# A convolution feeding a channel mix: how the later groups' x is loaded, when their units run, and when their output is written

## The chip, the cores and the metric

The kernel runs on one core of a Trainium2 chip. The metric is device time in microseconds, from the launch of the program to its end, as the median over several runs. TensorE (PE in the profile) multiplies, ScalarE (ACT) and VectorE (DVE) take results out of PSUM and do the elementwise work, GpSimd (POOL) and SyncE (SP) mostly issue DMAs.

## The reference, cut to what matters

```python
# first part: x (8, 4160, 192), weight (8 heads, 7 taps)
w = softmax(weight, axis=-1)
x_pad = concat(zeros(6 rows), x)                       # causal
y[b, s, head] = sum_k w[head, k] * x_pad[b, s + k, head]   # 24 channels per head
# second part, on y
y_prev = y shifted by one row
xk = mu_k * y + (1 - mu_k) * y_prev
xr = mu_r * y + (1 - mu_r) * y_prev
k = relu(xk @ w_k)                                     # 192 -> 1024
out = sigmoid(xr @ w_r) * ((k * k) @ w_v)              # 1024 -> 192
```

A depthwise causal convolution of seven taps, shared within each of eight heads, runs along the sequence. Its output goes through a channel mix: two blends of each row with the row before it, a 192 to 1024 to 192 network with a squared relu, and a sigmoid gate.

## The kernel before, in words

**Tiling.** The eight sequences are taken as four pairs p. A *step* is 512 rows of both sequences of a pair (there are 34, with short ones at the ends of the first pair and a last one for the tails). A step's k part is cut into *slots*, and four slots make a *bundle*: there are 65, and a step is two of them. Everything is issued by hand (`manual_schedule`): a loop over bundles b calls `bundle_first`, `bundle_second`, `bundle_third` and then `bundle_rest` for each. Each engine and each DMA queue runs its instructions in the order in which they are issued.

**A bundle** (`bundle_rest`). PE does four `k_mm` (ps_k, L591, 6 matmuls each), one `r` (ps_r, L648), one `v_rows` in two halves (ps_v, L679), and in some bundles a convolution unit. ACT does four `k_relu` (L603), one sigmoid (L659), and casts of the unit. DVE does four squares (L617), `v_out` (o_sb, L695) of the bundle before, and the blends: `diff` (d, L534), `scale` (L565), `add_y` (L571). `v_out` also has SP issue two DMAs to the output (L703). All PSUM results share one ring of four two-bank tiles, tag "k".

**Tables.** What a bundle does beside this stands in tables of calls by bundle: `early` runs ahead of the bundle, then `mix_a`, `mix_b` (after the first two k_mm), `mix_c`, and `late` at the end; `xt` holds the convolution units. `at(table, b, fn, ...)` adds a call.

**Groups.** The convolution is done in groups of blocks of rows. The first pair has six groups of other shapes (0 to 5). Pairs 1 to 3 have two groups each, 6 to 11, called *sparse*: 20 blocks of 4 x 26 rows, done with 32x32 matmuls (L362). `fb` is the bundle in which a group's first rows enter the channel mix; for groups 6 to 11 it is 16, 24, 32, 40, 48, 56. A sparse group goes through these stages:

1. `x_tile(g)` takes the next of two xb tiles and has DVE write two elements of it (L123), which waits for the tile's former users. `load_x(g, (s,))` has POOL issue four DMAs (L152) for sequence s, one for each quarter of the partitions, that read x in fp32 and write bf16. Before the second sequence, `tie_x` has DVE write two elements (L111) that the first of its DMAs overwrites, so that POOL waits for DVE to reach that place.
2. Four units c (`conv_sparse`), each with 32 matmuls over two PSUM tiles, and then ACT's casts (`cast_tiles`, L335) into two y tiles, one half of the rows each. The y tiles come from a pool of two, so the next group's first casts take the same two.
3. `y_write(g)` has SP issue eight DMAs (L464) that write y to a buffer in DRAM, four for each half.
4. `y_read` has SP issue two transposing DMAs (L486), one for each half of the rows, into yT, which `diff` reads from bundle fb - 2 on.

`keep_tail(p)` (y_tail, L518) copies the last rows of a pair's yT on POOL, in POOL's queue with the x loads.

**SP's queue** has all output writes, y writes and transposes in one order. After the last unit of a sparse group it holds: eight y writes, two output DMAs of the next `v_out`, two of the one after, the first transpose.

Of the kernel before, what the change touches and what calls it, by code (L numbers as in the profile page):

```python
# [14 lines left out]
def kernel(  # L15
# [11 lines left out]
    nc = tc.nc  # L27

    B, S, D = x.shape
# [11 lines left out]
    TB = 26  # L41
# [38 lines left out]
    n = 0  # L80
# [9 lines left out]
    groups = []  # L90
    for p in range(NPAIR):
        base = 0
        for nb, s, on_pe in (
# [4 lines left out]
            if on_pe is None:  # L98
                base = min(base, S - nb * 4 * TB)
# [3 lines left out]
    sparse = {g for g, grp in enumerate(groups) if grp[4] is None}  # L103
# [2 lines left out]

    xbs, homes = {}, {}

    def tie_x(g, s):

        nc.vector.memset(xbs[g][0:1, 1, s, 0:2], 0.0)  # L111

    def x_tile(g):
        p, base, nb, _, on_pe = groups[g]
# [12 lines left out]
            n0 = nb - (base + 2 * nb * HB - S) // HB - 1  # L127
            nc.gpsimd.memset(xb[Q:P, n0:nb, :, :], 0.0)

    def load_x(g, batches=range(2)):  # L130
        p, base, nb, _, on_pe = groups[g]
        xb = xbs[g]
        if on_pe:
            parts, step, rows = ((0, base),), BLK, P
        elif g in sparse:
            parts, step, rows = [(32 * i, base + i * nb * TB) for i in range(4)], TB, 32
        else:
            parts, step, rows = ((0, base), (Q, base + nb * HB)), HB, Q
        for s in batches:
            b = 2 * p + s  # L140
            for q0, start in parts:
                lo, hi = 0, nb
                t0 = start - HALO
                if t0 < 0:
                    lo = 1
                    nc.gpsimd.dma_start(out=xb[HALO:rows, 0, s, :], in_=x[b, 0 : rows - HALO, :])
                while t0 + (hi - 1) * step + HALO + step > S:
                    hi -= 1
                    r0 = t0 + hi * step
                    if r0 + HALO < S:  # L150
                        nc.gpsimd.dma_start(out=xb[q0 : q0 + S - r0, hi, s, :], in_=x[b, r0:S, :])
                nc.gpsimd.dma_start(  # L152
                    out=xb[q0 : q0 + rows, lo:hi, s, :],
                    in_=bass.AP(
                        tensor=x.tensor,
                        offset=x.offset + (b * S + t0 + lo * step) * D,
                        ap=[[D, rows], [step * D, hi - lo], [1, D]],
                    ),
                )
# [21 lines left out]
    n = groups[0][2] * 2 * D  # L181
# [118 lines left out]
    ys, yTs, y_drams = {}, {}, {}  # L300
# [149 lines left out]
    def new_yT(p):  # L450
        yTs[p] = two.tile([P, 3, -(-(YC + S) // 16) * 16], BF16, tag="yT", name="yT")
        y_drams[p] = dram.tile([NROW, 2 * D], BF16, tag=f"y{p % 2}", name="y_dram")
        nc.vector.memset(yTs[p][:, :, 0:YC], 0.0)


    def y_write(g):
        p, base, nb, _, _ = groups[g]
        if base == 0:
            new_yT(p)
        if g in sparse:  # L460
            m = nb // 4
            for half in range(2):
                for j in range(4):
                    nc.sync.dma_start(  # L464
                        out=bass.AP(
                            tensor=y_drams[p].tensor,
                            offset=y_drams[p].offset + (base + (2 * half * nb + j) * TB) * 2 * D,
                            ap=[[2 * D, TB], [4 * TB * 2 * D, 2 * m], [1, 2 * D]],
                        ),
                        in_=ys[g][half][32 * j : 32 * j + TB, :, :],  # L470
                    )
            return
        m = nb // 2
        for i in range(2):
            for j in range(2):
                r0 = base + (i * nb + j * m) * HB
                nc.sync.dma_start(
                    out=y_drams[p][r0 : r0 + m * HB, :].rearrange("(n t) c -> t n c", t=HB),
                    in_=ys[g][j * Q : j * Q + HB, i * m : (i + 1) * m, :],
                )  # L480

    def y_read(g, part=slice(0, 1), of=1):
        p, base = groups[g][:2]
        n = (ends[g] - base) // of
        r0, r1 = base + part.start * n, base + part.stop * n
        nc.sync.dma_start_transpose(  # L486
            out=yTs[p][:, :, YC + r0 : YC + r1], in_=y_drams[p][r0:r1, :]
        )
# [242 lines left out]
    early, rq, rs, xt, mix_a, mix_b, mix_c, vq, late = ({} for _ in range(9))  # L731

    def at(table, b, fn, *a):
        table.setdefault(b, []).append((fn, a))
# [7 lines left out]
    for g, (p, base, nb, fb, on_pe) in enumerate(groups):  # L742
        if g < 3:
            continue
        if p == 0:
            xs = {3: [1, 1], 4: [2, 2, 3, 3], 5: [4, 4, 5, 5]}[g]
        else:
            xs = {6: [7, 8, 9, 10], 7: [12, 13, 15, 17]}.get(g, [fb - 13, fb - 11, fb - 9, fb - 7])
        for i, b in enumerate(xs):
            xt.setdefault(b, []).append((g, i))  # L750
        if not on_pe:
            at(late, xs[-1], y_write, g)
        if g in sparse:
            at(late, max(fb - 5, xs[-1] + 2), y_read, g, slice(0, 1), 2)
            at(late, fb - 2, y_read, g, slice(1, 2), 2)
            b, b1 = {6: (3, 5), 7: (7, 9), 8: (15, 16), 9: (24, 25)}.get(g, (fb - 19, fb - 16))
            table = mix_c if g == 7 else early
            at(table, b, x_tile, g)
            at(table, b, load_x, g, (0,))
            table = mix_c if g == 6 else early  # L760
            at(table, b1, tie_x, g, 1)
            at(table, b1, load_x, g, (1,))
            continue
        if not on_pe:
            if g == 4:
                at(mix_c, 4, y_read, g, slice(0, 1), 2)
                at(late, 4, y_read, g, slice(1, 2), 2)
            else:
                at(late, 6, y_read, g)
        if g > 4:  # L770

            at(mix_a, 1, x_tile, g)
            at(mix_a, 1, load_x, g)
    for s, (p, t0, L, n0, ns) in enumerate(steps):
        fb = first_bundle[s]
# [27 lines left out]
    for s, j, vb in quads:  # L803
        b = vb - (s == LAST)
# [261 lines left out]
```

## Time and profile before

| | |
|---|---|
| median of 3 runs | 410.98 us (410.81 to 411.77) |
| profiled execution | 409.68 us |
| its span | 407.9 us |
| PE busy | 400.9 us, 98% |
| PE weight loads busy | 303.7 us, 74% |
| DVE busy | 369.5 us, 91% |
| ACT busy | 354.7 us, 87% |
| POOL busy | 57.9 us, 14% |
| moved by DMA | 66.23 MB, mean 162 GB/s |

The span is from the first to the last instruction that the profile holds; the execution is 1.8 us longer. Busy time is the union of an engine's instructions, DMA issues not counted. In lists of waits the numbers are the total in microseconds, how often, and the longest; in the chain and the timelines, the start, the duration and what ran, with how many instructions were put together.

### The profile page before, as it was taken

What the parts mean: (1) busy time and instruction counts of PE and PEld (TensorE: products, weight loads), DVE (VectorE), ACT (ScalarE), POOL (GpSimd) and SP (SyncE); (2) the same over time, 40 slices, a digit from 0 to 9 for tenths busy, and PEclk for the clock granted to TensorE, in tenths of its full rate; (3) what the DMA queues carried; (4) which work ended last, traced back from release to release, by engine and by line L of the source; (5) the groups of instructions that cost most, each with busy time, mean ns of one, the idle gap of its engine ahead of it and who ended that gap; (6) DMA issues with size and microseconds to landing.
All of it is one profiled execution on the core that took longest, in us unless ns stands there. A gap on an engine that the chain in (4) does not pass through costs nothing.

```text
span 407.9 us, 17547 instructions
## 1 busy us (share of the span) xinstructions
PE 400.9 (98%) x7736; PEld 303.7 (74%) x7736; DVE 369.5 (91%) x672; ACT 354.7 (87%) x426; POOL 57.9 (14%) x91
## 2 busy tenths in 40 slices
PE   8899999999999999999999999999999999999996
PEld 5667777767878777777777777777777778777795
DVE  5999899988999999999999999999999899999973
ACT  6899989989988898988898898889899877877781
POOL 8731223000700003104020013000000001000000
PEclk9999999999999999999999999999999999999999
DMA  9999999999997758999995896969623946221223
GB/s 151 188 204 227 191 213 208 219 215 193 161 192 208 169 125 140 221 221 187 192 166 141 224 184 126 167 179 213 120 80 97 218 119 159 79 77 43 80 80 116
DMA packets 138955, 66.23 MB, mean 162 GB/s; under 512 B 89356, under 2 KB 138880, under 8 KB 138880
## 3 DMA queue, kind: packets, MB, share of 16 engines
q1 hardware_dynamic: 95536, 48.20, 47.6%
q0 software_dynamic: 42544, 16.36, 34.9%
q8 instruction: 60, 0.98, 1.0%
q10 hardware_dynamic: 800, 0.57, 0.5%
q14 instruction: 15, 0.12, 0.1%
HBM read 33.29 MB, written 36.86 MB: 172 GB/s over the span
## 4 chain that ended last, share of the span: by engine, by line
PE 93%; ACT 1%; issue 0%; DVE 0%; ACTq 0%
PE ps_v L679 42%; PE ps_k L591 40%; PE ps_r L648 8%; PE ps_c L362 2%; PE ps_v L631 1%; ACT k_sb L603 1%; PE ps_c L317 0%; ACT y L437 0%; PE ps_c L391 0%; DVE o_sb L715 0%; ACTq L399 0%; ACTq L603 0%
## 5 line engine op out<-in xcount | busy, mean ns | idle before, releaser
L603 ACT ACTIVATE k_sb<-ps_k 128x1024 bf16<-128x1024 f32 x260 | 253.4, 1039 | 34.0 <-PE ps_k L591 33.2
L617 DVE TENSOR_TENSOR k<-k_sb 128x1024 bf16<-128x1024 bf16 x260 | 173.4, 688 | 25.7 <-ACT k_sb L603 25.7
L591 PE MATMUL ps_k<-xk,wk 64*128 64x512 bf16 (+1 forms) x1632 | 192.1, 367 | 0.9 <-DMA wk<-in_moe_w_k_dram 0.9
L679 PE MATMUL ps_v<-wv,k 64*128 64x192 bf16 x4032 | 188.8, 243 | 0.2
L679 PEld LDWEIGHTS <-k 64*128 64x128 bf16 x4032 | 168.6, 94 | 12.7 <-issue 5.0
L591 PEld LDWEIGHTS <-wk 64*128 64x128 bf16 x1632 | 84.8, 94 | 55.1 <-issue 1.4
L695 DVE TENSOR_TENSOR o_sb<-ps_v,r_sb 128x768 f32<-128x768 f32 x64 | 60.9, 951 | 2.7 <-issue 2.4
L152 POOL DMA_DIRECT2D xb<-in_x_dram x62 | 43.9, 714 | 135.4 <-DVE xb L111 48.8
L659 ACT ACTIVATE r_sb<-ps_r 128x768 bf16<-128x768 f32 x65 | 53.5, 825 | 7.7 <-PE ps_v L679 5.6
L335 ACT CAST y<-ps_c 128x960 bf16<-128x960 f32 (+2 forms) x84 | 52.6, 709 | 0.0
L648 PEld LDWEIGHTS <-xr 64*128 64x128 bf16 x780 | 35.0, 94 | 14.1 <-issue 0.4
L648 PE MATMUL ps_r<-wr,xr 64*128 64x192 bf16 x780 | 43.3, 243 | 0.0
L565 DVE TENSOR_SCALAR xr<-d,mu 128x512 bf16<-128x512 bf16 (+1 forms) x102 | 35.0, 347 | 0.0
L534 DVE TENSOR_TENSOR d<-yT 128x1536 bf16<-128x1536 bf16 (+4 forms) x36 | 31.2, 866 | 1.1 <-ACT yT L421 1.0
L571 DVE TENSOR_TENSOR xr<-xr,yT 128x1536 bf16<-128x1536 bf16 (+1 forms) x33 | 31.1, 942 | 1.1
L565 DVE TENSOR_SCALAR xk<-d,mu 128x512 bf16<-128x512 bf16 (+1 forms) x99 | 31.7, 350 | 0.1
L571 DVE TENSOR_TENSOR xk<-xk,yT 128x1536 bf16<-128x1536 bf16 (+3 forms) x33 | 30.5, 924 | 0.1
L518 POOL COPY y_tail<-yT 128x195 bf16<-128x195 bf16 x4 | 3.5, 868 | 89.5 <-DMA yT<-y_dram 89.5
L362 PEld LDWEIGHTS <-toe 32*32 32x32 bf16 x768 | 5.0, 88 | 10.3 <-issue 8.9
L362 PE MATMUL ps_c<-xb,toe 32*32 32x240 bf16 x768 | 10.9, 267 | 0.0
L125 POOL MEMSET xb<- 32x384 bf16 x3 | 1.2, 408 | 61.5 <-PE ps_v L679 34.2
L411 PE MATMUL ps_t<-toe,xb 128*32 128x120 bf16 (+3 forms) x264 | 5.4, 238 | 0.2 <-ACT yT L421 0.2
(60 smaller groups left out, 61.9 us busy)
## 6 DMA issues: line engine op xcount, KB each, us to landing
out_dram<-o_sb SPq DMA_DIRECT2D x128, 192.0 KB
xb<-in_x_dram POOLq DMA_DIRECT2D x52, 240.0 KB, 8.2
y_dram<-y SPq DMA_DIRECT2D x48, 195.0 KB
y_dram<-y SPq DMA_DIRECT2D x8, 210.0 KB
xb<-in_x_dram POOLq DMA_DIRECT2D x6, 228.0 KB, 4.6
xb<-in_x_dram POOLq DMA_DIRECT2D x4, 192.0 KB, 6.0
wk<-in_moe_w_k_dram POOLq DMA_DIRECT2D x4, 192.0 KB, 5.8
wv<-in_moe_w_v_dram POOLq DMA_DIRECT2D x1, 384.0 KB, 8.4
```

What stands on the lines that cost most here:

```text
L152: nc.gpsimd.dma_start(out=xb[q0 : q0 + rows, lo:hi, s, :], in_=bass.AP(tensor=x.tensor, offset=x.offset + (b * S + t0 + lo * step) * D, ap ...
L335: nc.scalar.copy(out=bass.AP(tensor=y.tensor, offset=y.offset + d, ap=[y.ap[0], [m * 2 * D, 2], [2 * D, m], [Q, 2], [1, b - a]],), in_=bas ...
L534: nc.vector.tensor_tensor(out=shaped(s, diffs[s][:, cs, :L]), in0=y_of(s, cs, 1), in1=y_of(s, cs, 0), op=ALU.subtract)
L565: nc.vector.tensor_scalar(out=t[:, c, :L], in0=diffs[s][:, c, :L], scalar1=mu[:, i, c : c + 1], scalar2=None, op0=ALU.mult)
L571: nc.vector.tensor_tensor(out=o, in0=o, in1=y_of(s, sl, 0), op=ALU.add)
L591: nc.tensor.matmul(out=ps[:, i, f * L : (f + 1) * L], lhsT=wk[r, c, fs], rhs=xk[r, c, :L], start=c == 0 and f == 0, stop=c == NC - 1 and f ...
L603: nc.scalar.activation(out=k_sb, in_=ps.rearrange("p a b -> p (a b)"), func=AF.Relu)
L617: nc.vector.tensor_tensor(out=o, in0=i, in1=i, op=ALU.mult)
L648: nc.tensor.matmul(out=ps[:, i, k * D : (k + 1) * D], lhsT=xr[q, c, ts], rhs=wr[q, c, :], start=c == 0, stop=c == NC - 1,)
L659: nc.scalar.activation(out=r_sbs[s, j], in_=r_ps.pop((s, j))[:, :, 0 : 2 * D], func=AF.Sigmoid)
L679: nc.tensor.matmul(out=v_ps[s, j][:, bank, k * D : (k + 1) * D], lhsT=k2s[s][q, f, t * P : (t + 1) * P], rhs=wv[q, f, :], start=half == 0 ...
L695: nc.vector.tensor_tensor(out=o_sb.rearrange("p (b t) d -> p b (t d)", b=2), in0=v_ps.pop((s, j)), in1=r_sbs.pop((s, j)), op=ALU.mult,)
```

## The change

Three things change for groups 6 to 11.

- x: the load is cut into its eight DMAs. `load_part(g, s, i)` has DVE write two elements of quarter i of sequence s, and POOL issue that quarter's DMA. Two parts are called in each of four consecutive bundles, one in `early` and one in `mix_b`. The start is bundle 3, 7, 14 for groups 6, 7, 8 and fb - 18 for the rest (before: two calls of four DMAs, at 3 and 5, 7 and 9, 15 and 16, 24 and 25, and fb - 19 and fb - 16).
- Units: group 6 stays at 7 to 10; the others are at fb - 12, fb - 10, fb - 8, fb - 6 (before: 12, 13, 15, 17 for group 7, and fb - 13, fb - 11, fb - 9, fb - 7).
- y: `y_write_half` writes one half with four DMAs, in `late` of fb - 6 and of fb - 5 (before: both halves in `late` of the last unit's bundle). The transposes are called at fb - 4 and fb - 2 (before: fb - 5, or 12 for group 6, and fb - 2).

```diff
-    def tie_x(g, s):
-
-        nc.vector.memset(xbs[g][0:1, 1, s, 0:2], 0.0)
+    def load_part(g, s, i):
+
+        nc.vector.memset(xbs[g][32 * i : 32 * i + 1, 1, s, 0:2], 0.0)
+        load_x(g, (s,), slice(i, i + 1))
...
-    def load_x(g, batches=range(2)):
+    def load_x(g, batches=range(2), which=slice(None)):
...
-            for q0, start in parts:
+            for q0, start in parts[which]:
...
+    def y_write_half(g, half):
+        p, base, nb, _, _ = groups[g]
+        if base == 0 and half == 0:
+            new_yT(p)
+        m = nb // 4
+        for j in range(4):
+            nc.sync.dma_start(
+                out=bass.AP(
+                    tensor=y_drams[p].tensor,
+                    offset=y_drams[p].offset + (base + (2 * half * nb + j) * TB) * 2 * D,
+                    ap=[[2 * D, TB], [4 * TB * 2 * D, 2 * m], [1, 2 * D]],
+                ),
+                in_=ys[g][half][32 * j : 32 * j + TB, :, :],
+            )
...
-            xs = {6: [7, 8, 9, 10], 7: [12, 13, 15, 17]}.get(g, [fb - 13, fb - 11, fb - 9, fb - 7])
+            xs = [7, 8, 9, 10] if g == 6 else [fb - 12, fb - 10, fb - 8, fb - 6]
...
-        if not on_pe:
+        if on_pe is False:
             at(late, xs[-1], y_write, g)
         if g in sparse:
-            at(late, max(fb - 5, xs[-1] + 2), y_read, g, slice(0, 1), 2)
-            at(late, fb - 2, y_read, g, slice(1, 2), 2)
-            b, b1 = {6: (3, 5), 7: (7, 9), 8: (15, 16), 9: (24, 25)}.get(g, (fb - 19, fb - 16))
-            table = mix_c if g == 7 else early
-            at(table, b, x_tile, g)
-            at(table, b, load_x, g, (0,))
-            table = mix_c if g == 6 else early
-            at(table, b1, tie_x, g, 1)
-            at(table, b1, load_x, g, (1,))
+            for half in range(2):
+                at(late, fb - 6 + half, y_write_half, g, half)
+                at(late, fb - 4 + 2 * half, y_read, g, slice(half, half + 1), 2)
+            b = {6: 3, 7: 7, 8: 14}.get(g, fb - 18)
+            at(early, b, x_tile, g)
+            for n in range(8):
+                at((early, mix_b)[n % 2], b + n // 2, load_part, g, n // 4, n % 4)
             continue
```

More of the change, by code (lines that the diff above doesn't have):

```diff
@@ L459, in y_write @@
             new_yT(p)
[L460 to L472, printed above, removed]
         m = nb // 2
```

## The prediction

> **What bounds the kernel now.** I read the page first: its busy row, slices and chain.
>
> ```profile
> span 407.9 us, 17547 instructions
> PE 400.9 (98%) x7736; PEld 303.7 (74%) x7736; DVE 369.5 (91%) x672; ACT 354.7 (87%) x426; POOL 57.9 (14%) x91
> ...
> DMA  9999999999997758999995896969623946221223
> ...
> PE 93%; ACT 1%; issue 0%; DVE 0%; ACTq 0%
> ```
>
> PE is busy 98% and makes up 93% of the chain, so time is lost only where PE is made to wait. The DMA engines are nearly full for the first 70% of the span, but nothing in the chain is a DMA. Next, PE's own waits:
>
> ```profile
> PE warm L851 <- DVE ones_t L830: 1.5, 1, 1.5
> PE ps_k L591 <- DMA wk<-in_moe_w_k_dram: 0.9, 2, 0.5
> PE ps_t L411 <- ACT yT L421: 0.2, 1, 0.2
> PE ps_c L317 <- ACT k_sb L603: 0.2, 1, 0.2
> ```
>
> That is the whole list, 2.8 us, all of it before bundle 4: the 32x32 groups make PE wait nowhere. Busy PE need not be PE at its peak, so I read its pace from the chain of waits in order of time. A run of 18 ps_k matmuls opens each bundle:
>
> ```profile
> 186.00 1.94 PE ps_k L591 x18
> ...
> 192.20 2.00 PE ps_k L591 x18
> ...
> 197.98 1.94 PE ps_k L591 x18
> ...
> 204.18 2.00 PE ps_k L591 x18
> ...
> 317.46 1.94 PE ps_k L591 x18
> ...
> 323.21 1.94 PE ps_k L591 x18
> ```
>
> Bundles take 6.20 and 5.78 us in turn where every second one holds a unit, and 5.74-5.75 at the end where none does and DMA is quiet. A pair with a unit takes 11.98, so a unit costs 11.98 - 2 x 5.74 = 0.50 us, its own matmuls (0.35-0.50 in the chain, and a few hundredths of slower ps_v). There is no wait in the loaded stretch to give back. Here the Trainium skill speaks for more room: "Trainium Kernel Development and Optimization", Performance Expectations, says that matmul busy time is a bad measure and weight-load busy a good one. By it, 74% leaves a quarter to gain. By the pace, identical with DMA full and with DMA quiet, there is about none. I take the pace.
>
> Last, the engines around one hand-over of the y tiles (group 9's last unit, then group 10's first), from the timelines of SP, ACT and PE:
>
> ```profile
> 216.31 7.41 SPq L464 DMA_DIRECT2D y_dram<-y  x8
> 223.82 2.97 SPq L703 DMA_DIRECT2D out_dram<-o_sb  x4
> 226.83 4.47 SPq L486 DMA_TRANSPOSE yT<-y_dram  x1
> ```
> ```profile
> 215.33 1.82 ACT L335 CAST y<-ps_c 128x960 bf16<-128x960 f32 x2
> ...
> 227.25 1.82 ACT L335 CAST y<-ps_c 128x960 bf16<-128x960 f32 x2
> ```
> ```profile
> 215.99 2.11 PE L591 MATMUL ps_k<-xk,wk 64*128 64x512 bf16 x18
> ```
>
> SP issues eight y writes, about 0.95 us each[...], then two out pairs, then the transpose. The casts of the next group's first unit, 11.9 us later, write the same two y tiles (pool of two) and must wait for those writes. The PE row matters as much: its 18 matmuls are three ps_k tiles of 0.65 us (a run of six in the chain), so the third starts at 217.29; the PSUM ring has four tiles and this one takes the tile that the second cast has just left (215.33 + 1.82 = 217.15). PE's margin behind that cast is 0.14 us.
>
> **The change, part by part.**
>
> *Memsets.* Eight ties per sparse group instead of one, six groups: 42 more DVE memsets at 59 ns (the tile view of xb) = 2.5 us of DVE over 24 loading bundles, two to a bundle. DVE is busy 44.3 of 47.8 us between 198.66 and 246.46, so 0.5 us more fits the 3.5 idle. The work that is put back by 0.06-0.12 us is the square, xk and o_sb; xk of the next step is ready at 202.3 and first read at 204.18, 1.9 us later (0.7 in a bundle without a unit). Cost 0; if that cover is gone, 0.12 us a loading bundle, 2.5 in all.
>
> *x in eight parts.* The same 62 transfers, 0.69 us each on POOL's queue, now each behind its own memset. The first waits for the previous tenant's loads as before. The last part goes out in the middle of bundle b+3, three bundles before the unit in the general case, against a landing of 7.8 us median and 14.4 at most: covered. The tight one is group 6: last part in bundle 6 (memset near 48 us, issued to 49), unit at 56.96. Before, the four DMAs behind the memset at 44.23 landed 5.2 to 8.9 us after issue, the last at 55.6. Now the others are already through, so I expect 54-56: nothing, bound 0 to 1 us. On POOL, y_tail of pair 0 moves between group 8's parts; the yT it needs is tens of us old there. Queue neighbours of the y writes change little: x is clear of them either way, except at group 6, where one or two parts are in flight before and after.
>
> *Units.* Groups 7 to 11 move by 0 or 1 bundle, so pairs stay pairs. Group 7's first two units no longer stand side by side: bundles 12 to 18 take 6.20, 6.33, 5.73, 6.40, 5.78, 6.48, 5.73 in the chain, 42.65 - 7 x 5.74 = 2.47 for four units, against 4 x 0.50. Gain 0 to 0.5; I take 0.3. In the even bundles DVE carries a little more (o_sb, xr, d), but the long bundle gives it 0.45 us more.
>
> *y_read.* SP's order was y x8, out, out, transpose; it becomes y x4, out, y x4, out, transpose. The same twelve DMAs stand ahead of the transpose, so it starts 9.7-10.8 us after the last cast as before and lands 17-18 after it (before: 226.83 + 4.47, landing counted at 234.9 by the trace's semaphore records). But units end one bundle nearer to the reader, d (L534) in bundle fb-2: 5.7 + 6.2 + 5.7 to its first relu and 2.7 into it = about 20 us after the cast, where it was 26. Margin 2-3 us, no cost taken.
>
> *y_write in halves.* This is where I see a price. The second half goes out "a bundle later", but SP is paced by its queue: the first four writes keep it until about 3.1 us after the cast, then the out pair of the next v_out, whose o_sb is ready by then, then at once the second four. What changes is one out pair ahead of four of the eight writes: the pair's issues took 1.3, 1.4, 1.3, 1.9 and 2.7 us (with their semaphore waits 1.4, 1.5, 1.4, 2.0, 2.8) in the five hand-overs. Bound below: the pair is free in the queue, 0. Nothing in the trace shows a second half behind a pair, so I use the landing records: the eighth y write landed at 88.61, 131.56, 179.75, 227.11 and 275.80, and the second cast that needs it began at 89.86, 132.50, 180.29, 228.09 and 275.90, so the slack was 1.25, 0.94, 0.54, 0.98, 0.10. With the pair's issue time added, it is late by 0.1, 0.6, 0.9, 1.0, 2.7; by the landing of the tenth DMA instead (88.61 becomes 89.67; 132.74; 180.82; 229.30; 276.77) by -0.2, 0.2, 0.5, 1.2, 0.9. Less PE's margin of 0.14 each: 4.7 us and 2.3 us. The rule that stands here is in "DMA: Bandwidth & Descriptors", Anatomy of one DMA: about 2.0 us plus bytes over 436 GB/s, given there for the GpSimd path, which makes 2.5 us for a 195 KB write. The trace has 3.2 to 4.1 us from the end of the eighth issue to its landing, behind a full queue. With the rule the lateness falls by 0.7-1.6 each and about 1.0 us is left; I keep the trace. ACT catches up from its idle time (0.82 + 0.21 a pair), PE cannot: it has none. I take 2.7.
>
> Sum: -0.3 + 0 + 0 + 2.7 = +2.4 us on the profiled 409.7 (407.9 span and 1.8 around it). The median of the runs is 410.98, 1.3 above the profiled execution; I add the difference to it: 413.4.
>
> **Rivals.** *It lands in time (0.30).* Without x beside them the writes drain faster, and the out pair costs less than the slack of 0.1-1.25 plus 0.14. Then only the spacing is left, -0.5 to 0: 410.5-411.0, no change. For it: the slack is real in four of five places, and DMA is only 0.74 busy between 268 and 272 us. Against: SP's 0.95 us a write[...]. It decides at a second half that lands under 11.9 us after the first half's issue began; 12.1-12.3 is my reckoning.
>
> *A late input (0.08).* Group 6's last part stops PE at bundle 7, or the transpose misses d: each microsecond past a 2-3 us margin, four times, goes through DVE to xk and PE. 414-418.
>
> *Faster (0.07).* Timed runs are 1.3 us above the profiled one; if that is DMA bursts that the profile did not catch, spreading x would give part of it back: 409.5.
>
> That the parts are not spread at all is unlikely: POOL did wait for the ties, six times, 48.8 us in all.
>
> **How the numbers follow.** Forecast, the late second half: 0.55, 411.8 to 416.0. A measurement tells about 0.3% from nothing, 1.2 us. Of the forecast 0.03 falls inside that, so slower is 0.52 + 0.08 = 0.60, same 0.33, faster 0.07. The range goes from the no-change case with its gain, 410.2, to the upper sum, 416.0.
>
> **What would show it.** Right: ACT idle before L335 casts, released by the DMA y_dram<-y, up to five times, 0.2-2 us, all in first units, and PE waiting for ACT at ps_k right after; SP rows of four y writes with two outs between. Wrong: no such wait and pairs still at 11.95; or waits of PE or DVE on xb or yT instead.

## The result, and the profile after

The changed kernel takes 430.52 us, the median of six runs (427.14 to 436.09), against 410.89 for the kernel before in the same comparison (six runs, 410.65 to 414.08): a ratio of 1.0454, interval 1.0394 to 1.0514. It is slower by 19.6 us, where 2.4 had been forecast. Every kernel here has some executions more than 1.5% above its fastest; the ratios leave these out, and where a median below contains some, the times behind its ratio stand beside it. The profiled execution took 433.16 us with a span of 431.5, so it is 2.6 us above the median; the accounts below are of this execution, against the 407.9 us of span before.

The head of the page of the changed kernel: span, busy row, chain by engine.

```profile
span 431.5 us, 17622 instructions
...
PE 404.4 (94%) x7736; PEld 304.2 (71%) x7736; DVE 375.0 (87%) x714; ACT 355.6 (82%) x426; POOL 57.0 (13%) x91
...
PE 49%; DVE 21%; DMA 9%; ACT 6%; SPq 5%; issue 5%; DVEq 0%; ACTq 0%
```

PE's busy time grew by only 3.5 us while the span grew by 23.6, so PE now waits for some 20 us. It makes up 49% of the chain that ended last, where it was 93%, and DMA, which had no share at all, has 9%. What PE waited for (total, how often, longest):

```profile
PE ps_k L594 <- ACT y L336: 6.9, 5, 1.7
PE ps_k L594 <- DVE xk L574: 5.4, 1, 5.4
PE ps_v L682 <- issue: 3.1, 3, 1.6
PE ps_k L594 <- DMA wk<-in_moe_w_k_dram: 2.4, 3, 1.0
PE ps_r L651 <- DVE o_sb L698: 1.7, 1, 1.7
```

The first row is the predicted wait, at all five hand-overs of the y tiles. The second is a single wait of 5.4 us, of a kind that the prediction gave a chance of 0.08. The third has no releaser in the profile; the last section comes back to it. To place them I measured each bundle from the start of its first relu to that of the next, before and after:

| bundles | before, us | after, us | difference |
|---|---|---|---|
| ahead of bundle 0 | 11.41 | 12.57 | +1.2 |
| 6 | 5.67 | 13.58 | +7.9 |
| 7 to 10 | 25.31 | 29.89 | +4.6 |
| 12, 20, 28, 36, 44 (hand-overs) | 5 x 6.38 | 40.14 | +8.2 |
| 32 | 6.48 | 7.50 | +1.0 |

For the hand-overs and bundle 32, the column "before" has the undisturbed length in a kernel with the units of the changed one (a_y_whole_x67 below). The rows make 22.9 of the 23.6 us. The first belongs to no part of the change: the code is the same there, PE waits for the load of wk, and the kernels of the experiments show 12.0 to 12.7 there whatever they change.

The row of bundles 7 to 10 needs the same caution, since "before" is one execution. Four kernels below have the code of the kernel before up to bundle 10 (b_units, b_y_halves, b_y_halves_pool, b_x8_parts); they take 26.2 to 29.6 us there, and in each `d` waits 1.6 to 3.2 us for group 5's transpose. So 0.9 to 4.2 us can be lost in these bundles without any change to them.

Elsewhere the pace is the old one. The chain of waits in order of time, of the changed kernel, has the same runs of 18 ps_k matmuls 6.20 and 5.77 us apart in turn:

```profile
310.84 1.94 PE ps_k L594 x18
317.04 2.00 PE ps_k L594 x18
322.81 1.94 PE ps_k L594 x18
```

So two places carry the loss: the hand-overs of y (8.2) and bundles 6 to 10 (12.5, of which 7.9 in bundle 6).

**A hand-over.** Group 9 to group 10 again, timelines of SP, ACT and PE of the changed kernel (start, duration, what ran, idle time before it and its releaser):

```profile
242.03 3.00 SPq L476 DMA_DIRECT2D y_dram<-y  x4
245.14 2.67 SPq L706 DMA_DIRECT2D out_dram<-o_sb  x2
247.91 3.90 SPq L476 DMA_DIRECT2D y_dram<-y  x4
251.91 2.69 SPq L706 DMA_DIRECT2D out_dram<-o_sb  x2
254.63 3.83 SPq L489 DMA_TRANSPOSE yT<-y_dram  x1
```
```profile
252.98 0.95 ACT L336 CAST y<-ps_c 128x960 bf16<-128x960 f32 x1
255.82 0.96 ACT L336 CAST y<-ps_c 128x960 bf16<-128x960 f32 x1 [1.89 <-PE ps_k L594]
```
```profile
253.64 1.46 PE L594 MATMUL ps_k<-xk,wk 64*128 64x512 bf16 x12
256.83 0.82 PE L594 MATMUL ps_k<-xk,wk 64*128 64x512 bf16 x6 [1.73 <-ACT y L336]
```

The order on SP is the predicted one, and PE stops at the third ps_k tile of the bundle, behind the second cast, as was worked out from the PSUM ring. The cast starts 4.0 us after the last y issue ended (251.81 to 255.82). Its idle time is put down to PE, whose matmuls had ended at 255.10; in two of the five it is put down so, in the other three to the DMA `y_dram<-y`. The releaser is inferred, and the edits below decide which it is.

**Bundles 3 to 6.** SP's queue, the kernel before and then the changed kernel:

```profile
35.06 2.69 SPq L477 DMA_DIRECT2D y_dram<-y  x4
37.85 1.60 SPq L703 DMA_DIRECT2D out_dram<-o_sb  x2
39.56 4.00 SPq L486 DMA_TRANSPOSE yT<-y_dram  x2
...
47.79 2.09 SPq L477 DMA_DIRECT2D y_dram<-y  x4
```
```profile
36.35 2.61 SPq L465 DMA_DIRECT2D y_dram<-y  x4
39.06 3.34 SPq L706 DMA_DIRECT2D out_dram<-o_sb  x2
42.51 11.67 SPq L489 DMA_TRANSPOSE yT<-y_dram  x2
54.24 1.45 SPq L706 DMA_DIRECT2D out_dram<-o_sb  x2
55.73 4.78 SPq L465 DMA_DIRECT2D y_dram<-y  x4
```

These are group 4's y writes and its two transposes, and then the y writes of group 5: the pair before the sparse groups, which the diff does not touch. The transposes held SP for 11.67 us instead of 4.00. At the same time POOL sent x loads, one at a time, where before nothing left it for 12.3 us, until SP had both transposes out. POOL's timeline, before and then after:

```profile
44.61 2.73 POOL L152 DMA_DIRECT2D xb<-in_x_dram  x4 [12.30 <-DVE xb L111]
```
```profile
42.24 0.86 POOL L153 DMA_DIRECT2D xb<-in_x_dram  x1 [2.42 <-DVE xb L111]
44.07 0.69 POOL L153 DMA_DIRECT2D xb<-in_x_dram  x1 [0.97 <-DVE xb L111]
47.37 0.68 POOL L153 DMA_DIRECT2D xb<-in_x_dram  x1 [2.62 <-DVE xb L111]
49.80 0.68 POOL L153 DMA_DIRECT2D xb<-in_x_dram  x1 [1.75 <-DVE xb L111]
```

The stretch from 38 to 56 us, before and then after (length; busy time and instructions of PE, PEld, DVE, ACT, POOL; granted clock; DMA share; GB/s):

```profile
38.00:56.00 18.00, 18.00 (x328) 13.13 (x326) 16.56 (x30) 16.75 (x21) 2.73 (x4) 1.00 1.16 225
```
```profile
38.00:56.00 18.00, 16.29 (x305) 12.01 (x300) 10.54 (x23) 15.34 (x20) 4.09 (x6) 1.00 1.37 148
```

The DMA share (the packets' time as a share of the engines' time) rose, and the bytes moved fell by a third. The two transposes landed at 57.18 and 64.65 instead of 44.1 and 47.38, and DVE's `d` of the next step waited for the first (timeline of DVE, and the same wait in the chain, changed kernel):

```profile
57.20 0.96 DVE L537 TENSOR_TENSOR d<-yT 128x1536 bf16<-128x1536 bf16 x1 [7.70 <-DMA yT<-y_dram]
```
```profile
42.51 14.66 DMA yT<-y_dram
```

SP was held behind it, so group 5's y went out at 55.73 instead of 47.79, its transpose landed at 83.6 instead of 67.3, and `d` waited 4.2 us for it in bundle 9.

Of bundle 6's 7.9 us, the wait for xk is 5.4 and a stop without a releaser 1.55; the rest is a half clock (last section), which reaches into bundle 7. In bundles 7 to 10 PE then waits 1.4 us at another such stop and 1.7 us for o_sb, which DVE brings late after its wait for group 5.

### The profile page after: what moved, and what is told of

It is laid out like the page before. It is cut to its first block, busy times and chain, and to the rows that moved or that the text cites. A ratio compares the mean times of both kernels' runs of the same rounds, so it can differ in the third digit from the quotient of the medians.

```text
span 431.5 us, 17622 instructions
## 1 busy us (share of the span) xinstructions
PE 404.4 (94%) x7736; PEld 304.2 (71%) x7736; DVE 375.0 (87%) x714; ACT 355.6 (82%) x426; POOL 57.0 (13%) x91
## 4 chain that ended last, share of the span: by engine, by line
PE 49%; DVE 21%; DMA 9%; ACT 6%; SPq 5%; issue 5%; DVEq 0%; ACTq 0%
PE ps_v L682 21%; PE ps_k L594 21%; DVE k L620 7%; DMA y_dram<-y 5%; ACT k_sb L606 4%; PE ps_r L651 4%; DVE o_sb L698 4%; DMA yT<-y_dram 3%; SPq L706 3%; SPq L476 2%; DVE xk L568 2%; DVE d L537 2%; DVE xr L574 2%; DVE xk L574 2%; DVE xr L568 2%
## 5 line engine op out<-in xcount | busy, mean ns | idle before, releaser
L594 PE MATMUL ps_k<-xk,wk 64*128 64x512 bf16 (+1 forms) x1632 | 195.1, 369 | 14.7 <-ACT y L336 6.9
L594 PEld LDWEIGHTS <-wk 64*128 64x128 bf16 x1632 | 85.7, 94 | 71.0 <-issue 11.9
L521 POOL COPY y_tail<-yT 128x195 bf16<-128x195 bf16 x4 | 2.6, 649 | 84.7 <-DMA yT<-y_dram 84.7
L634 PE MATMUL ps_v<-wv,k 128*128 128x192 bf16 x64 | 5.5, 246 | 0.0
```

The lines of the kernel that those rows point to most:

```text
L594: nc.tensor.matmul(out=ps[:, i, f * L : (f + 1) * L], lhsT=wk[r, c, fs], rhs=xk[r, c, :L], start=c == 0 and f == 0, stop=c == NC - 1 and f ...
```

## The experiments

Two theories stood at first. One: the hand-overs cost about 8 us because of the place of the second y half, and bundles 6 to 10 about 12 because x parts of groups 6 and 7 run beside the transposes of groups 4 and 5. The rival: the late landings have another source (the moved units, or the loads' extra ties), and taking the x parts away only moves them.

### Undoing one part of the change

**Both y halves together again (a_y_whole).**

```diff
-                at(late, fb - 6 + half, y_write_half, g, half)
+                at(late, fb - 6 if g > 6 else 10, y_write_half, g, half)
```

> The changed kernel with both halves of y written together, at the end of the last unit's bundle, as before; x parts, unit places and transposes as changed. Theory (two separate costs): the second half behind an output pair made ACT wait 1.2 to 1.9 us at five hand-overs, 7.7 us, and that goes: 422 to 423 us, no idle time before the casts at the five first units, pairs of bundles at 11.95 from bundle 16 on, while bundles 6 to 10 stay long by some 12 us. Rival (the spread x loads slow the y writes themselves): the casts still wait about a microsecond each, 427 us or more.

Measured: 426.56 us (four runs, 421.72 to 428.85; behind the ratio 421.72 and 424.39) against 412.02, ratio 1.027 (1.0199 to 1.0341). Bundles 12, 20, 28, 36 and 44 all take 6.38. The row of five PE waits for the cast is gone, so its cause is shown: it is the place of the second half. The ratio falls by 1.8%, about 7.6 us, close to the 8.2. The profiled execution (428.73 us) has bundle 6 at 13.27 and bundles 9, 10 and 32 at 8.68, 8.60 and 8.50 (7.80, 8.27 and 7.50 in the changed kernel), with waits that nothing in the profile releases:

```profile
PE ps_v L682 <- issue: 7.4, 3, 3.8
```

**x of groups 6 and 7 loaded as before (a_x67).** The old `tie_x` comes back as well.

```diff
...
             b = {6: 3, 7: 7, 8: 14}.get(g, fb - 18)
+            if g < 8:
+                b, b1 = {6: (3, 5), 7: (7, 9)}[g]
+                table = mix_c if g == 7 else early
+                at(table, b, x_tile, g)
+                at(table, b, load_x, g, (0,))
+                table = mix_c if g == 6 else early
+                at(table, b1, tie_x, g, 1)
+                at(table, b1, load_x, g, (1,))
+                continue
```

> The changed kernel with x of groups 6 and 7 loaded in two calls of four DMAs as before (bundles 3 and 5, 7 and 9); groups 8 to 11 stay in eight parts. Theory: the parts of these two groups run beside the transposes of groups 4 and 5, which then land 13 to 16 us later and stop DVE's d: that goes, bundles 6 to 10 fall back to 5.7 to 6.4 us, 418 to 420 us, with the five waits of ACT left. Rival (eight ties and eight separately started DMAs cost in every group): only a third of the 12 us goes, 426 us.

Measured: 425.31 us (419.55 to 429.68, four runs; behind the ratio 419.55 and 422.35) against 412.02, ratio 1.0219 (1.0146 to 1.0291). Bundles 6 to 10 take 5.67, 6.38, 6.29, 6.33 and 6.22, what they took before, while the hand-overs stay (7.57 to 8.44). Both as the theory had it, and the ratio falls by 2.4%, about 9.7 us. In the profiled execution (429.68 us) bundles 15, 16 and 32 take 10.66, 7.97 and 10.52, with two PE gaps of 3.70 and 2.62 us without a releaser, each with a half clock (see the last section).

**x of group 6 alone as before (a_x6).** The same edit with `g == 6`.

> The changed kernel with x of group 6 alone in two calls as before. Theory: group 6's parts delay group 4's transposes, these hold up SP's queue, so y of group 5 is written and transposed late: all of the loss in bundles 6 to 10 starts there, and the time is that of the kernel with both groups put back, 418 to 420 us. Rival (group 7's parts delay group 5's transpose by themselves): bundle 6 is back at 5.7 us but bundles 7 to 10 stay long by 3 to 5 us, 422 to 424 us.

Measured: 423.87 us (421.69 to 428.86, four runs; behind the ratio 421.69 to 423.92), ratio 1.0272 (1.0219 to 1.0325). Bundle 6 is back to 5.67: its loss is group 6's. Bundles 7 and 9 stay at 7.30 and 7.95, and the time is the rival's. That the rest is the parts of group 7 is not shown, though: bundles 7 to 10 take 28.1 us here, and 26.2 to 29.6 in the four kernels whose code is unchanged there.

**Both undone (a_y_whole_x67).** The two edits above together; the parts for groups 8 to 11, the places of the units and the transposes stay as changed.

> The changed kernel with both put back: y written whole, x of groups 6 and 7 in two calls. Left of the change: x of groups 8 to 11 in eight parts, units in every second bundle, transposes at fb - 4. Theory: the two costs are all, 410 to 411.5 us, ratio 0.998 to 1.001. Rival (the rest costs as well, by 42 memsets or by the later transposes): 412 to 415 us.

Measured: 414.91 us (20 runs, 411.57 to 421.66; behind the ratio 411.57 to 417.52) against 412.02, ratio 1.0058 (1.0036 to 1.0080). Most of the loss is gone, but what is left is slower than the kernel before and not the gain that the theory allowed. The ratios close the sum: 4.5% for the whole change, less 1.8% for y and 2.4% for x of groups 6 and 7, leaves 0.3%, and 0.6% was measured. In the profiled execution (412.59 us) all bundles are normal but bundle 10 (7.39) and, by a stop of 0.95 us without a releaser, bundle 15. DVE's one long wait is in bundle 9, for group 5's transpose, where the code is that of the kernel before:

```profile
DVE d L541 <- DMA yT<-y_dram: 2.5, 1, 2.5
```

What the 0.6% consists of stays open.

### One part of the change alone, in the kernel before

**Only the y halves (b_y_halves).** With `y_write_half` of the changed kernel.

```diff
...
-            at(late, xs[-1], y_write, g)
+            for half in range(2):
+                at(late, xs[-1] + half, y_write_half, g, half)
```

> The kernel before with only the writing of y changed: the second half a bundle after the first, so that an output pair stands between them in SP's queue. Theory: ACT waits at the five first units for y_dram<-y, 1.2 to 1.9 us each, PE with it, and nothing else changes: 417.5 to 419.5 us on a before of 411, ratio 1.017 to 1.021. Rival (the wait needs the moved x loads as well): under 413 us.

Measured: 420.01 us (418.81 to 420.5, four runs) against 411.66, ratio 1.0192 (1.0154 to 1.0229), as expected. PE's list of waits and SP at the hand-over to group 10:

```profile
PE ps_k L593 <- ACT y L335: 6.2, 5, 1.7
```
```profile
223.01 3.01 SPq L475 DMA_DIRECT2D y_dram<-y  x4
226.12 2.67 SPq L705 DMA_DIRECT2D out_dram<-o_sb  x2
228.89 3.39 SPq L475 DMA_DIRECT2D y_dram<-y  x4
```

The pair behind four y writes takes 2.67 us here too, with the x loads and the units of before: neither sets its price.

**Only the x parts (b_x_parts).** The loads of all six groups by the changed kernel's table and its `load_part`, the rest as before.

```diff
...
-            b, b1 = {6: (3, 5), 7: (7, 9), 8: (15, 16), 9: (24, 25)}.get(g, (fb - 19, fb - 16))
...
-            at(table, b, load_x, g, (0,))
...
-            at(table, b1, load_x, g, (1,))
+            b = {6: 3, 7: 7, 8: 14}.get(g, fb - 18)
+            at(early, b, x_tile, g)
+            for n in range(8):
+                at((early, mix_b)[n % 2], b + n // 2, load_part, g, n // 4, n % 4)
```

> The kernel before with only the x loads changed: eight parts over four bundles in all six groups, units and y as before. Theory: bundles 6 to 10 lose 9 to 13 us through the late transposes of groups 4 and 5, DVE's d idle for up to 8 us before DMA yT<-y_dram; groups 8 to 11 lose at most 2 us: 421 to 424 us. Rival (it is the parts together with the moved units or y writes): 412 to 415 us.

Measured: 424.90 us (422.91 to 427.13, four runs) against 411.66, ratio 1.0322 (1.0280 to 1.0363), just above the expectation: the largest of the three parts. Later groups lost more than expected: bundles 15 and 16 take 15.96 instead of 12.17, with a stop of 1.69 us without a releaser and a half clock. Bundle 6 takes 13.20, and group 4's transposes hold SP as in the changed kernel, without a moved unit or y write:

```profile
43.31 11.09 SPq L491 DMA_TRANSPOSE yT<-y_dram  x2
```

**Only the units and the transposes' places (b_units).**

```diff
-            xs = {6: [7, 8, 9, 10], 7: [12, 13, 15, 17]}.get(g, [fb - 13, fb - 11, fb - 9, fb - 7])
+            xs = [7, 8, 9, 10] if g == 6 else [fb - 12, fb - 10, fb - 8, fb - 6]
...
-            at(late, max(fb - 5, xs[-1] + 2), y_read, g, slice(0, 1), 2)
+            at(late, fb - 4, y_read, g, slice(0, 1), 2)
```

> The kernel before with only the places of the units and the first transposes changed (fb - 12, -10, -8, -6; transpose at fb - 4). Theory: the spacing is worth 0 to 0.5 us and the later transposes still land before d: 410.5 to 411 on 411, ratio 0.998 to 1.0005; if so it is the version that may beat both. Rival (the later transposes or the even bundles cost): 412 us or more, with DVE's d or PE's ps_r waiting.

Measured: 417.97 us (six runs, 414.22 to 423.61; behind the ratio 414.22 to 418.64) against 411.66, ratio 1.0116 (1.0073 to 1.0158). A miss: I had expected nothing or a small gain. The gain is there: bundles 12 to 18 take 42.3 us instead of 42.6. The loss stands elsewhere. SP of this kernel around bundle 38, then DVE and PE:

```profile
237.27 5.12 SPq L486 DMA_TRANSPOSE yT<-y_dram  x1
...
247.01 10.54 SPq L486 DMA_TRANSPOSE yT<-y_dram  x1
```
```profile
250.01 0.96 DVE L534 TENSOR_TENSOR d<-yT 128x1536 bf16<-128x1536 bf16 x1 [1.57 <-DMA yT<-y_dram]
```
```profile
251.61 0.65 PE L679 MATMUL ps_v<-wv,k 64*128 64x192 bf16 x11 [1.57 <-issue]
```

POOL had sent four x loads from 238.57 on, beside the first of these transposes and ahead of the second. The margin of 2 to 3 us failed once, by the 1.57 us that `d` waits for the first; the second, which keeps SP for 10.54 us, is waited for by nobody. PE's list has no wait for xk, so the late `d` is not shown to have cost anything. What PE did lose after bundle 10 is two stops without a releaser, 1.57 us here and 1.68 at 267.84, in bundles 38 and 41 (4.2 us in bundles 38 to 41 against a_y_whole_x67). Another 4.2 us of this execution lies in bundles 7 to 10, where nothing was changed. So the cause of the 1.2% stays open in part.

The three parts alone add up to 6.3%, the whole to 4.5%. The parts may share losses; in the changed kernel, whose loads start at other bundles than here, all transposes of groups 6 to 11 came in time.

### Which property of the x parts costs

The theory was now: not the cutting and not the ties, but loads under way beside group 4's two transposes.

**Group 6 only, the second call of four moved to bundle 4 (b_x6_early).** Four loads as one burst, one tie, no parts.

```diff
-            b, b1 = {6: (3, 5), 7: (7, 9), 8: (15, 16), 9: (24, 25)}.get(g, (fb - 19, fb - 16))
+            b, b1 = {6: (3, 4), 7: (7, 9), 8: (15, 16), 9: (24, 25)}.get(g, (fb - 19, fb - 16))
...
-            table = mix_c if g == 6 else early
+            table = early
```

> The kernel before with one thing moved: the second call of group 6's x (four DMAs behind one tie) goes from mix_c of bundle 5 to the start of bundle 4, so that it runs beside group 4's transposes; nothing is cut in parts. Theory (it is x beside the transposes, however it is cut): the transposes land late, d waits, bundle 6 gets longer by several us: 416 to 421 us. Rival (the cutting and the eight ties do it): bundle 6 stays at 5.7 us, 411 us.

Measured: 416.04 us (six runs, 413.63 to 418.72) against 411.66, ratio 1.0101 (1.0063 to 1.0138). Nothing is cut and no tie is added, yet the two transposes are slow again, after a burst that left POOL at 36.80 to 39.55 (SP):

```profile
41.38 10.71 SPq L486 DMA_TRANSPOSE yT<-y_dram  x2
```

Bundle 6 takes 8.41 instead of 5.67. So the place of the loads alone brings the slow transposes; the time lost is smaller than with the parts: `d` waits 3.3 us here, where it waits 7.7 in the changed kernel. That this is because the burst was through sooner is likely, not shown.

**Group 6 only, in eight parts (b_x6_parts).** The edit of b_x_parts under `if g == 6`.

> The kernel before with x of group 6 alone in eight parts over bundles 3 to 6. Theory: SP's two transposes of group 4 take 10 to 12 us instead of 4.0 as in the run with all groups in parts, d waits 7 us, and most of the loss of that kernel is here: 418 to 422 us. Rival (group 7's parts carry half of it): 415 to 417 us.

Measured: 421.10 us (419.80 to 426.33, four runs; behind the ratio 419.80 to 421.12) against 412.16, ratio 1.0207 (1.0162 to 1.0251), as expected. Bundle 6 takes 12.30, SP's transposes 10.94 us. One group of six is most of the 3.2% of b_x_parts.

**Groups 8 to 11 in parts (b_x8_parts).** The same under `if g > 7`.

> The kernel before with x of groups 8 to 11 in eight parts, 6 and 7 as before. Theory: their parts meet one transpose each with slack before d, so only late instruction loads of PE are left: 411.5 to 414 us, no DVE wait on yT over 1 us. Rival (the parts cost the same in every group): 417 us or more.

Inconclusive: four runs of 413.64, 414.00, 421.22 and 426.62 us give no ratio; the two lower ones lie in the theory's 411.5 to 414. The profiled execution, the first of these, has bundle 6 at 5.67, and its transposes of group 4 take SP 3.65 us, with no parts beside them. Its later transposes do have parts beside them and take 5.70 to 7.99 us each, but no `d` waits for them: its only wait for yT, 1.8 us, is for group 5 in bundle 9.

**All eight loads of group 6 in one burst at bundle 3 (b_x6_burst).** If only loads beside the transposes cost, an earlier burst should be clear of them.

```diff
...
+            if g == 6:
+                at(table, b, load_x, g, (1,))
+                continue
...
```

> The kernel before with both calls of group 6's x at the start of bundle 3, eight DMAs in a row, so that most of x has landed before group 4's first transpose is issued. Theory (place, not number): the transposes take under 7 us on SP, d waits 0 to 2 us: 411 to 413 us. Rival (any earlier x costs since the DMA engines are full): 415 us or more.

Measured: 414.17 us (20 runs, 412.45 to 416.68) against 412.16, ratio 1.0060 (1.0038 to 1.0083), between the theory and the rival. The transposes come later, at 45.60, and take 6.29 us, and `d` waits 2.8. The earlier the loads were sent, the less was lost, but it does not come to nothing: SP waited 5.1 us for group 4's y writes to land before the first transpose could go. The two bursts had gone out just ahead of those writes (30.84 to 36.85).

SP's time for group 4's two transposes, over all kernels: 3.57 to 4.13 in the eight with group 6's x as before, 6.29 (burst at 3), 10.71 (burst at 4), and 10.46 to 11.67 in the four with parts in bundles 3 to 6.

The later transposes of the changed kernel agree. Four single ones have x parts beside them and take 5.76 to 7.39 us of SP; those of groups 6 to 11 with none take 3.32 to 4.33. The slowest:

```profile
213.28 7.39 SPq L489 DMA_TRANSPOSE yT<-y_dram  x1
```

Nothing waited for these, so they cost nothing by themselves. How much a transpose loses does not follow from the loads' place alone: with four loads sent 6 to 8 us ahead of it, one took 4.44 us in the kernel before (at 242.09) and one 10.54 in b_units (at 247.01), and with four sent just after its start one took 3.48 in the kernel before (at 57.52).

### Which property of the y halves costs

**The out pair between the halves on another queue (b_y_halves_pool).** b_y_halves, with the output pair of bundles 11, 18, 26, 34 and 42 issued by POOL, so that SP has eight y writes in a row; the rest of the edit is that of b_y_halves. If SP's order is the cause, the waits go; if the pair's demand on the DMA engines is, they stay.

```diff
...
-            nc.sync.dma_start(
+            (eng or nc.sync).dma_start(
...
-                v_out(*vq[b - 1][0])
+                v_out(*vq[b - 1][0], nc.gpsimd if b in (11, 18, 26, 34, 42) else None)
```

> The kernel with y in halves alone, and in addition the output pair that stood between the halves is issued from POOL's queue (five bundles: 11, 18, 26, 34, 42), so that SP's queue has the eight y writes in a row again. Theory A (it is the order of SP's queue): the ACT waits at the hand-overs go, 411 to 413 us. Theory B (it is what the pair takes of the DMA engines, whatever queue it is on): the waits stay at 0.8 us or more each, 416 us or more.

Measured: median 421.82 us over nine runs (414.67 to 424.09; behind the ratio four, 414.67 to 417.54) against 412.16, ratio 1.0093 (1.0059 to 1.0128). PE's wait and SP at the same hand-over as above:

```profile
PE ps_k L593 <- ACT y L335: 3.7, 5, 1.3
```
```profile
221.76 8.51 SPq L475 DMA_DIRECT2D y_dram<-y  x8
```

Neither theory alone holds. The wait falls from 6.2 to 3.7 us, 40%, and the eight writes now take SP 8.51 us where they took 7.41 before. So the pair slows them from another queue too; by what is not shown.

No edit points to a version that beats the kernel before: each one measured was slower than it, or gave no ratio.

## Why the prediction was wrong

**The direction and one mechanism were right.** Slower, through a second y half that lands after the cast wants the tile: five times, only in first units, at the third ps_k tile, with ACT able to catch up and PE not. This is not luck, as b_y_halves has that loss alone (1.9%). That pace and not weight-load busy time says how much room PE has held too: away from the named places, bundles kept their 6.20 and 5.77 us.

**Mis-sized: "What changes is one out pair ahead of four of the eight writes".** The pair was priced by where it stood before, behind eight y writes, at 1.3 to 2.7 us, and this led to 2.7 us in all. Behind four writes it took 2.67 to 2.82 in all five places; with 2.7 each, the prediction's own sum gives 9.0 us. At the hand-over shown, the last y issue ended 251.81 - 242.03 = 9.78 us after the first began, against 7.41 before: 2.4 later, where the sum had 1.9. The landing, by the semaphore records, came 3.9 us behind it (255.68), against 3.4 (223.72 to 227.11): 0.5 more. Together 2.9, less the slack of 0.98, is 1.9, and 1.89 of idle time was measured. At all five, the second half landed 13.0 to 13.7 us after the first issue, not the reckoned 12.1 to 12.3, with 7.7 us of cast idle and 8.2 us of bundle time. The choice between the trace and the rule (the Trainium skill, "DMA: Bandwidth & Descriptors", Anatomy of one DMA: 2.0 us plus bytes over bandwidth) was right: the rule would have moved the sum further off, to 1.0.

**The step that failed: "x in eight parts ... covered ... nothing, bound 0 to 1 us".** I asked only whether the parts land before group 6's unit, which they did: the unit is not where PE waits. I did not ask what the parts run beside, but for the y writes. In bundles 3 to 6 they run beside two transposes that `d` of bundle 6 needs. Those took 11.67 us of SP instead of 4.00 and landed 13 and 17 us later; `d` waited 7.7 us and PE 5.4. The trace before showed all that was needed to ask: the two transposes at 39.56, and POOL sending nothing from 32.3 us until 44.61, when SP had issued them. That gap was the cover, and the change filled it. It cost 2.4% by a_x67 (groups 6 and 7), and 2.1% with the parts of group 6 alone in the kernel before. In the account by bundles it is the 7.9 us of bundle 6 and a part of the next 4.6.

**A cost with no term: PE's stops without a releaser.** Four of them over 0.5 us make 4.5 us of the changed kernel's 23.6, and the profile before had none (last section).

**What held.** The margin of 2 to 3 us for the moved transposes was enough in the changed kernel: `d` waits there for groups 4 and 5 only, which the change does not move. The spacing of the units gave its 0.3 us in b_units. That kernel is nevertheless 1.2% slower, which no term of the prediction has. The memsets, forecast at no cost, are not where the slow transposes come from: b_x6_early has none added and shows them too.

**The range** ended at 416.0, the upper end of the forecast alone. The "late input" rival, priced at 414 to 418 by "each microsecond past a 2-3 us margin", came true beside it in kind: a transpose missed `d`, though of group 4 and with a wait of 7.7 us. The two mechanisms were weighed as alternatives, and they add up.

## What to carry to other kernels

When a load is spread or moved, check for each new place which transfers of other queues are under way there and what their margins are; that the load meets its own deadline says nothing about them. A gap in a queue next to a DMA transpose may be its cover. A short transfer that is put between two parts of a longer one on the same queue costs what it takes there (2.7 us here), not what it took at the end (1.3 to 2.7), and moving it to another queue gave only part of that back (40% of the wait here). A profile of one execution can be a lucky one: compare a stretch with kernels that have the same code there before a loss in it is put down to the change.

## What was not expected of the hardware

**Transposes beside casting loads.** A pair of DMA transposes took 4.00 us of SP's queue, or 10.5 to 11.7 with fp32-to-bf16 loads from POOL's queue beside them, a factor of 2.6 to 2.9. That a transpose also stops its queue is what carried the delay to group 5. The fall to 148 GB/s is not tied to it: b_x6_early, with 10.71 us for the pair, moved 212 GB/s in the same stretch. Which resource the two share, and whether loads without a cast do the same, no run here shows.

**The clock falls to half, in pieces of 3.41 us.** After the 5.4 us of idle PE, the changed kernel's granted clock is 0.5 for 3.41 us from 61.19 on (stretch of 61 to 65 us):

```profile
61.00:65.00 4.00, 3.79 (x24) 1.50 (x26) 3.88 (x11) 2.03 (x2) 1.36 (x2) 0.57 0.96 217
```

That costs about 3.41 / 2 = 1.7 us, in bundles 6 and 7. The Trainium skill, "TensorE: Matmul & The Clock Gate", Part 1, gives a window of about 3.4 us, after which an idle PE gets half the clock until a busy window has passed; the length agrees. But the fall came after shorter gaps too, such as 2.62 us in a_x67 and 1.77 in b_units, and did not come after one of 2.28 in a_y_whole. The traces show what decides beside the length: within each, the falls stand on a fixed grid. They are 109.23 us apart in a_x67, 61.44 in b_x_parts and 44.37 in b_x6_burst, which is 32, 18 and 13 times 3.413. So a gap's place on the grid counts, and the same kernel can have the fall in one execution and not in another (mean clock 0.988 to 0.995 in the changed kernel's six runs, 1.000 in the profiled one of a_x6).

**PE's stops with no releaser are waits for its instructions.** In the changed kernel and its relatives PE stops for 0.6 to 3.8 us without any wait that the profile shows, as at 51.90 and 225.90 in the changed kernel. The page has a DMA queue of the kind "instruction":

```profile
q8 instruction: 60, 0.98, 0.9%
```

That is 60 packets for 15,500 matmuls and weight loads, about one for 256. All 26 such stops over 0.5 us after the first 12 us of the 14 traces come at one place of the count, 192 or 193 past a multiple of 256. Each ended 2.3 to 3.6 us after a packet of this queue began, and in the 826 times that PE passes such a place it never did so sooner than 2.2 us after the packet began. In the 26 cases the packet had begun 4.1 to 7.6 us after PE passed the place before; past 345 us, where the DMA engines are quiet, the median is 0.1 us. So late instructions stop PE, and crowded DMA engines as the reason for the lateness fit, but no edit here tests that.
